# Whole 128x128 float32 products for the last two batches' linear attention, in front of two feed-forward layers

## Chip, cores and metric

The kernel runs on one core of a Trainium2 chip. The metric is the device time of one execution in microseconds, as the median of several runs. Engines are named as in the profile: PE is TensorE's products and PEld its weight loads, DVE is VectorE, ACT is ScalarE, POOL is GpSimd, SP is the engine that issues most DMAs.

## What is computed

Random-feature attention for 4 batches, 8 heads, 576 positions and a head size of 64 with 128 features, then two feed-forward layers over all 2304 tokens (512 to 2048 to 512), everything in float32:

```python
def phi(x):
    proj = np.einsum('bhsd,md->bhsm', x, omega)
    h = proj - np.sum(x * x, axis=-1, keepdims=True) / 2.0
    h = h - np.max(h, axis=-1, keepdims=True)
    return np.exp(h) / np.sqrt(m)
kv = np.einsum('bhsm,bhsd->bhmd', k_p, v)
z = np.sum(k_p, axis=2)
num = np.einsum('bhsm,bhmd->bhsd', q_p, kv)
den = np.einsum('bhsm,bhm->bhs', q_p, z)[..., None] + 1e-06
attn = num / den
# then x @ w_in, h * clip(h + 3, 0, 6) / 6, @ w_out
# then x @ w_in, h * sigmoid(1.702 h), @ w_out
```

## The kernel before

**Tiles.** The 576 positions of a head are four blocks of 128 (R = 4) and 64 leftover positions (SL). Values carry a 65th column of ones (D + 1 = 65), so that the product of key features and values gives `kv` and `z` together, and the product of query features with that gives numerator and denominator together. Leftover positions of the two heads of a pair share one tile: the first head's keys (and values, in `lv`) on rows 0 to 63, the second's on rows 64 to 127.

**Stages.** The first batch's attention runs alone at the start. From then on the attention of batch n + 1 is cut into steps (`att_steps`), and the steps are put between the products of the first feed-forward layer for batch n: `side()`, called in the middle and at the end of every chunk of `emit_h` and `emit_o`, takes steps from the list `todo` at an even pace. So the third batch's attention lies within the layer's work on the second batch (about 193 to 295 us), the fourth's within that on the third (about 307 to 417 us). The first layer's products with w_in are L459, those with w_out L510, both 128x128 weights against 512 columns in reduced float32 split into high and low parts. The second layer (L811, L828, L942) starts near 558 us. A scheduler that simulates the engines sets the order of the instructions on each engine from the order in which the kernel gives them, and each engine then runs in that order.

**Steps of one batch's attention.** For h from 0 to 9, in this order: `PJ(h)` projects keys and queries of head h (L259, two row halves side by side) and takes maxima and exponentials; after it, for h = 0, `PL` does so for the leftovers and, for h = 2, `QTL` transposes the leftover queries of all heads (L293); `NU(h - 2)` makes numerators and denominators (L354) and, for odd heads, those of the pair's leftovers (L363), then normalises (`norm`: L376, L380, L381 on DVE); `QT(h - 1)` transposes query features (L337) and `KV(h - 1)` makes the key-value sum (four blocks at L315, leftovers at L323, copied by ACT at L331); for odd h from 3 on, `XT` transposes the finished pair (L392) and splits it for the feed-forward layer (L247, L248); at the end `XTL` transposes the leftovers (L399).

**What the change touches.** Key-value sums and numerators are done in column halves: `KV` loads weight columns 0 to 63 and 64 to 127 of the features as two products that write PSUM rows 0 to 63 and 64 to 127, and `NU` does the same with the query features. The leftover product of `KV` takes 64 rows and 64 columns at a time. The accumulators come from a ring of four PSUM banks (`bank`, pool `psp`) that `emit_h` and the attention share. `load_left` issues the leftover loads on SP (`lqk`, and `lv` at L119); `kv` tiles come from a ring of four.

Of the kernel before, what the change touches and what calls it, by code (L numbers as in the profile page):

```python
# [8 lines left out]
F32 = mybir.dt.float32  # L9
# [13 lines left out]
def performer_moe_kernel(  # L23
# [13 lines left out]
    nc = tc.nc  # L37
# [4 lines left out]
    B, NPAIR, P = qk.shape[:3]  # L42
    H = 2 * NPAIR
    R = v.shape[4]
    D = omega.shape[0] // 2
    M = omega.shape[1]
    SM = R * P
    SL = lv.shape[1] // 2
# [6 lines left out]
    TAIL = 12  # L55
    WARM = 8
    FIRST = 4
    HELD = 8
    LOOK = 5
    PREP = 9  # L60
# [23 lines left out]
    def bank(shape, name):  # L84
        n_ps[0] += 1
        if banks[0] == "acc" or banks[0] == "both" and n_ps[0] % 2:
            return acc.tile(shape, F32, tag="acc", name="acc")
        return psp.tile(shape, F32, tag="ps", name="ps")
# [6 lines left out]
        return stack  # L95


    qkv = {}
    lqkv = {}
    last_load = [None]  # L100
# [13 lines left out]

    def load_left(b):
        a = at.tile([P, NPAIR, P], F32, tag="lqk", bufs=1, name="lqk")
        vl = at.tile([P, NPAIR, D + 1], F32, tag="lv", bufs=2, name="lv")
        nc.sync.dma_start(out=a, in_=lqk[b])
        nc.sync.dma_start(out=vl, in_=lv[b])  # L119
        lqkv[b] = (a, vl)  # L120

    w_dram = ((w1_in, w1_out), (w2_in, w2_out))
# [124 lines left out]
        nc.scalar.copy(hi, ps)  # L247
        nc.vector.tensor_tensor(out=lo, in0=ps, in1=hi.bitcast(F32), op=ALU.subtract)  # L248

    HALVES = (slice(0, D), slice(D, 2 * D))  # L250

    def project(a, ps):

        last = None
# [17 lines left out]
    class Att:  # L272


        def __init__(self, b, x, xl):
            self.b, self.x, self.xl = b, x, xl
            self.e, self.kv, self.xt, self.feat, self.qt = {}, {}, {}, {}, {}

        def leftover(self, i, j):
# [27 lines left out]
            return self.e[h][:, r % 2, 2 * j + r // 2]  # L307

        def KV(self, h):
            i, p0 = h // 2, 64 * (h % 2)  # L310
            vv = qkv[self.b, i][1]
            ps = bank([P, D + 1], "ps")
            for r in range(R):
                for m0 in (0, 64):
                    nc.tensor.matmul(  # L315
                        out=ps[m0:m0 + 64, :],
                        lhsT=self.feature(h, 0, r)[:, m0:m0 + 64],
                        rhs=vv[:, h % 2, r, :],
                        start=(r == 0),
                        stop=False,  # L320
                    )
            for m0 in (0, 64):
                nc.tensor.matmul(  # L323
                    out=ps[m0:m0 + 64, :],
                    lhsT=self.leftover(i, 1)[p0:p0 + SL, m0:m0 + 64],
                    rhs=self.vl[p0:p0 + SL, i, :],
                    start=False,
                    stop=True,
                )
            kv = at.tile([P, D + 1], F32, tag="kv", bufs=4, name="kv")  # L330
            nc.scalar.copy(kv, ps)  # L331
            self.kv[h] = kv

# [11 lines left out]
        def NU(self, h):  # L345
            i = h // 2
            t = self.qt.pop(h)
            kv = self.kv[h]
            if h % 2 == 0:
                self.xt[i] = at.tile([P, R, 2, D], F32, tag="xt", bufs=1, name="xt")  # L350
            ps = bank([P, 6, D + 1], "ps")
            for r in range(R):
                for s0 in (0, 64):
                    nc.tensor.matmul(  # L354
                        out=ps[s0:s0 + 64, r, :],
                        lhsT=t[:, r, s0:s0 + 64],
                        rhs=kv,
                        start=True,
                        stop=True,
                    )  # L360
            if h % 2:
                for e in range(2):
                    nc.tensor.matmul(  # L363
                        out=ps[0:SL, R + e, :],
                        lhsT=self.qtl[:, i, 64 * e:64 * e + SL],
                        rhs=self.kv.pop(2 * i + e),
                        start=True,
                        stop=True,
                    )
            self.norm(ps[:, 0:R, :], self.xt[i][:, :, h % 2, :], P, R)  # L370
            if h % 2:
                self.norm(ps[0:SL, R:R + 2, :], self.xln[:, i], SL, 2)

        def norm(self, ps, dst, np_, n):
            d = at.tile([P, R, 1], F32, tag="den", bufs=3, name="den")
# [29 lines left out]
    def att_steps(a):  # L405
        b = a.b
        st = []
        for h in range(H + 2):
            if h < H:
                st.append(lambda h=h: a.PJ(h))  # L410
            if h == 0:
                st += [lambda: None] * 2 + [lambda: a.PL()]
            if h == 2:
                st.append(lambda: a.QTL())
            if 2 <= h:
                st.append(lambda h=h: a.NU(h - 2))
            if 1 <= h <= H:
                st.append(lambda h=h: a.QT(h - 1))
                st.append(lambda h=h: a.KV(h - 1))
                if h % 2 == 0:  # L420
                    st.append(("load", (h - 1) // 2))
            if 2 <= h and h % 2:
                st.append(lambda h=h: a.XT((h - 2) // 2))
        st.append(lambda: a.XTL())
        fin = []
        for s in st:
            if isinstance(s, tuple):
                i = s[1] + 2
                bb, i = b + i // NPAIR, i % NPAIR
                if bb < B:  # L430
                    prev = fin.pop()

                    def f(prev=prev, bb=bb, i=i):
                        prev()
                        load_pair(bb, i)
                        if i == 0:
                            load_left(bb)
                    fin.append(f)
            else:
                fin.append(s)  # L440
        return fin
# [8 lines left out]
    def emit_h(n, c, side):  # L450
        w = ws[0, "i", c].rearrange("p s (k f) -> p s k f", k=NK)
        for i, N in SEGS[n]:
            pool = lp if i == B else gp
            x = xblk[i]
            ps = psp.tile([P, N], F32, tag="ps", name="ps")
            m = 0
            for kk in range(NK):
                for wi, xi in ((0, 0), (0, 1), (1, 0)):
                    nc.tensor.matmul(  # L459
                        out=ps,  # L460
                        lhsT=w[:, wi, kk, :],
                        rhs=x[:, xi, kk, :],
                        start=(m == 0),
                        stop=(m == 3 * NK - 1),
                    )
# [13 lines left out]
            if i == n:  # L479
                late_at("next")  # L480
                late_at("gate")
            hgt[i, c] = s
            side()
# [155 lines left out]
    for n in range(WARM):  # L639
        nc.tensor.matmul(  # L640
            out=ps.rearrange("p a m -> p (a m)"),
            lhsT=zero_r,
# [119 lines left out]
    for u in range(len(units) + LAG):  # L762
        while fetches and fetches[0][0] <= u + AHEAD:
            fetch_w(0, *fetches.pop(0)[1:])
        if u < len(units):
            n, c = units[u]
            if c == 0 and n + 1 < B:
                xblk[n + 1] = new_x(n + 1)
                steps = att_steps(Att(n + 1, xblk[n + 1], xl))
                todo = steps[::-1]  # L770
                pace[:] = len(todo), 0, 8 * (n > 0)
            if (n, c) == (B - 2, NC - 1):
                while todo:
                    todo.pop()()
                actx.close()
                lp = ctx.enter_context(
                    tc.tile_pool(name="lp", bufs=1, side="right", reuse_waits="tile")
                )
                xblk[B] = new_x(B)
                for kk in range(NK):  # L780
                    split_x(xl, xblk[B], kk)
            if n > 0:
                before_chunk(n, c)
            emit_h(n, c, side)
            if n == 0:
                convert_next(2, min(c + 2, NC), *(att.feat[H - 1] if c == 0 else ()))
            if (n, c) == (B - 1, PREP):
                assert n_late[0] == len(late)
                prep, _ = x_ops(0, wp, "w")
            if c == NC - 1:  # L790
                while todo:
                    todo.pop()()
        if u >= LAG:
            emit_o(*units[u - LAG], side)
# [343 lines left out]
```

## Time and profile before

| | us |
|---|---|
| median of 3 runs | 927.65 (926.71 to 927.83) |
| the profiled execution | 928.67 |
| its span, first to last instruction | 926.9 |
| TensorE products busy | 909.7 |
| TensorE weight loads busy | 772.0 |
| VectorE / ScalarE / GpSimd busy | 553.1 / 477.8 / 320.9 |

Times in rows count from the start of the span. A group of rows gives engine, line, operation, out<-in by the kernel's names, weight rows*columns, shapes, and how many. Products are pipelined: one record is longer than the step from its start to the next one's start, so steps are read from starts, or from a group's length less its last record.

### The profile page before, as it was taken

The numbers are of one execution on the slowest core, as the hardware profiler recorded it, in microseconds if no ns is written. First come the engines' busy times: TensorE is split into PE (matmuls) and PEld (weight loads), VectorE is DVE, ScalarE is ACT, GpSimd is POOL, SyncE is SP. The second block draws the span as 40 slices with busy tenths as digits, with TensorE's granted clock in tenths as the row PEclk, the third lists the DMA queues.
The fourth block names the chain that finished last, engine by engine and source line by source line (L and its number), as shares of the span: only waits on it lengthen the run. The fifth ranks groups of instructions, "written<-read, shape, count | busy, mean of one in ns | idle before, by whom it ended". The sixth has DMA issues, their size and how long they took to land.

```text
span 926.9 us, 16527 instructions
## 1 busy us (share of the span) xinstructions
PE 909.7 (98%) x6346; PEld 772.0 (83%) x6346; DVE 553.1 (60%) x944; ACT 477.8 (52%) x969; POOL 320.9 (35%) x251
## 2 busy tenths in 40 slices
PE   8899999999999999999999999999999999999997
PEld 6677777787777787778888888778999888899997
DVE  5877787463754836557563433776875443377653
ACT  6877676375664776646543333444544323244443
POOL 0122222054736557364772112884000244420000
PEclk9999999999999999999999999999999999999999
DMA  7677679687888998676866436999889544566572
GB/s 243 205 240 262 220 259 308 240 302 262 290 280 284 340 307 296 238 266 247 294 216 227 136 112 238 355 404 309 273 295 328 196 171 160 179 185 184 169 262 92
DMA packets 75167, 228.77 MB, mean 247 GB/s; under 512 B 7504, under 2 KB 13264, under 8 KB 75088
## 3 DMA queue, kind: packets, MB, share of 16 engines
q1 hardware_dynamic: 74928, 227.45, 71.5%
q8 instruction: 50, 0.82, 0.4%
q10 hardware_dynamic: 160, 0.26, 0.1%
q14 instruction: 29, 0.24, 0.1%
HBM read 164.77 MB, written 62.91 MB: 246 GB/s over the span
## 4 chain that ended last, share of the span: by engine, by line
PE 87%; DVE 5%; ACT 4%; DMA 2%; POOL 1%; issue 1%; DVEq 0%; SPq 0%; ACTq 0%
PE o L510 21%; PE ps L459 20%; PE o L942 20%; PE h L811 14%; PE ps L259 3%; PE hl L828 2%; ACT e L267 2%; PE ps L315 1%; PE ps L354 1%; PE ps L337 1%; DVE w L204 1%; DVE mx L265 1%; DMA fac<-xf 1%; DVE wtop L189 1%; PE ps L392 1%
## 5 line engine op out<-in xcount | busy, mean ns | idle before, releaser
L459 PE MATMUL ps<-x,wss 128*128 128x512 f32 x768 | 195.1, 399 | 0.9 <-ACT wss L207 0.6
L942 PE MATMUL o<-wss,gs 128*128 128x256 f32 x1536 | 185.2, 283 | 0.1
L942 PEld LDWEIGHTS o<-wss,gs 128*128 128x128 f32 x1536 | 184.5, 191 | 0.9 <-DVE gs L913 0.5
L459 PEld LDWEIGHTS ps<-x,wss 128*128 128x128 f32 x768 | 140.8, 189 | 33.4 <-ACT wss L207 2.0
L811 PE MATMUL h<-xo,wss 128*128 128x512 f32 x672 | 160.3, 394 | 1.0 <-DVE t L844 0.9
L811 PEld LDWEIGHTS h<-xo,wss 128*128 128x128 f32 x672 | 124.2, 188 | 28.9 <-DVE t L844 1.7
L196 POOL TENSOR_TENSOR w<-w,wpow 128x1024 f32<-128x1024 f32 x32 | 69.6, 2175 | 207.3 <-DVE wpow L193 166.4
L471 DVE SCALAR_TENSOR_TENSOR ga<-ga,ps 128x512 f32<-128x512 f32 (+1 forms) x80 | 49.7, 630 | 135.1 <-ACT ga L470 135.1
L852 POOL TENSOR_TENSOR g<-g,c 128x512 f32<-128x512 f32 x48 | 64.6, 1348 | 171.5 <-ACT g L851 171.3
L510 PE MATMUL o<-gs,wsh 128*128 128x512 f32 (+1 forms) x480 | 112.6, 377 | 0.8 <-ACT gs L475 0.8
L912 ACT CAST gs<-g 128x512 fp32r<-128x512 f32 x112 | 69.4, 621 | 85.1 <-PE o L942 79.3
L510 PE MATMUL o<-gs,wss 128*128 128x512 f32 (+1 forms) x480 | 110.4, 375 | 0.1
L221 POOL TENSOR_TENSOR wsn<-w,wsn 128x512 fp32r<-128x512 f32 x64 | 88.6, 1399 | 59.4 <-ACT wsn L220 58.4
L913 DVE TENSOR_TENSOR gs<-g,gs 128x512 fp32r<-128x512 f32 x112 | 79.7, 715 | 47.9 <-ACT gs L912 45.0
L470 ACT ACTIVATE ga<-ps,three 128x512 f32<-128x512 f32 (+1 forms) x80 | 51.2, 648 | 101.2 <-PE ps L459 100.8
L510 PEld LDWEIGHTS o<-gs,wsh 128*128 128x128 f32 x480 | 82.5, 188 | 18.0 <-ACT gs L475 1.1
L510 PEld LDWEIGHTS o<-gs,wss 128*128 128x128 f32 x480 | 82.2, 188 | 15.7 <-ACT gs L475 0.3
L476 DVE TENSOR_TENSOR gs<-ga,gs 128x512 fp32r<-128x512 f32 (+1 forms) x80 | 58.6, 742 | 18.4 <-ACT gs L475 17.0
L267 ACT ACTIVATE e<-ps,mx 128x128 f32<-128x128 f32 x220 | 61.4, 397 | 14.7 <-DVE mx L265 14.7
L851 ACT ACTIVATE g<-c 128x512 f32<-128x512 f32 x48 | 30.3, 632 | 62.7 <-DVE c L844 62.7
L475 ACT CAST gs<-ga 128x512 fp32r<-128x512 f32 (+1 forms) x80 | 46.0, 580 | 26.9 <-DVE ga L471 26.9
L204 DVE TENSOR_TENSOR w<-w,wtop 128x512 f32<-128x512 f32 x64 | 54.1, 890 | 7.4 <-POOL w L196 7.4
(127 smaller groups left out, 1084.1 us busy)
## 6 DMA issues: line engine op xcount, KB each, us to landing
wss<-left SPq DMA_DIRECT2D x64, 512.0 KB, 3.9
wss<-ws0i SPq DMA_DIRECT2D x48, 512.0 KB, 5.2
wraw<-in_w_in_dram SPq DMA_DIRECT2D x32, 512.0 KB, 5.6
wraw<-in_w_out_dram SPq DMA_DIRECT2D x32, 512.0 KB, 6.5
left<-wsn SPq DMA_DIRECT2D x32, 512.0 KB, 3.8
wss<-ws0o SPq DMA_DIRECT2D x24, 512.0 KB, 4.7
ws0i<-wss SPq DMA_DIRECT2D x16, 512.0 KB, 3.4
wss<-sumsa SPq DMA_DIRECT2D x16, 512.0 KB, 4.0
```

Of the source, the lines that this page charges most:

```text
L196: nc.gpsimd.tensor_tensor(out=w, in0=w, in1=q, op=ALU.mult)
L204: nc.vector.tensor_tensor(out=wj, in0=wj, in1=a[:, j * DM:(j + 1) * DM], op=ALU.add)
L221: nc.gpsimd.tensor_tensor(out=s[:, :, 1], in0=t, in1=s[:, :, 0].bitcast(F32), op=ALU.subtract)
L267: act = nc.scalar.activation(out=e[:, r, :], in_=ps[:, r, :], func=AF.Exp, bias=mx[:, r:r + 1])
L459: nc.tensor.matmul(out=ps, lhsT=w[:, wi, kk, :], rhs=x[:, xi, kk, :], start=(m == 0), stop=(m == 3 * NK - 1),)
L476: gate[1] = nc.vector.tensor_tensor(out=s[:, 1, :], in0=g, in1=s[:, 0, :].bitcast(F32), op=ALU.subtract)
L510: nc.tensor.matmul(out=ps[:, e, :], lhsT=w[:, wi, cols], rhs=s[:, gi, :], start=(c == 0 and m == 0 and per == 1), stop=(c == NC - 1 and m ...
L811: nc.tensor.matmul(out=ps, lhsT=s[:, wi, q, :], rhs=xop[q, op][:, xi], start=(first and m == 0), stop=(m == 5), skip_group_check=not first,)
L852: mul = eng.tensor_tensor(out=g, in0=g, in1=src, op=ALU.mult)
L912: split_ins[0] = nc.scalar.copy(s[:, 0], g)
L913: split_ins[1] = nc.vector.tensor_tensor(out=s[:, 1], in0=g, in1=s[:, 0].bitcast(F32), op=ALU.subtract)
L942: last_row[0] = nc.tensor.matmul(out=out, lhsT=s[:, gi, d * P:(d + 1) * P], rhs=w[:, wi, :], start=(start and m == 0), stop=(stop and m == 2),
```

## The change

For batches from `WHOLE` = 2 on (the third and the fourth), `KV` multiplies all 128 feature columns at once, and its leftover product takes all 128 rows: the other head's rows meet zeros in the values. For that the leftover values of a pair lie in two tiles `lvs`, one per parity of the batch, with a place for each head of a pair; both are zeroed once by GpSimd behind the fifth chunk of the first batch, and the values are loaded into them by two DMAs of 64 rows. `NU` multiplies 128 positions at once. The leftover numerators leave `NU` and become the step `NL`, four heads each, behind `NU(3)` and `NU(7)`, with one normalisation over four heads; the ring of `kv` grows from 4 to 10 for it. The first two batches keep their column halves.

```diff
+    WHOLE = 2
+    lvs = [at.tile([P, 2, NPAIR, D + 1], F32, name=f"lv{k}") for k in range(2)]
     def load_left(b):
...
+            vl = lvs[b % 2]
+            for e, rows in enumerate(HALVES):
+                nc.sync.dma_start(out=vl[rows, e], in_=lv[b, rows])
     def KV(self, h):
...
+            if self.whole:
+                cols, rows, vl = (slice(0, P),), slice(0, P), self.vl[:, h % 2, i, :]
+            else:
+                cols, rows = HALVES, HALVES[h % 2]
+                vl = self.vl[rows, i, :]
             for r in range(R):
-                for m0 in (0, 64):
+                for m in cols:
                     nc.tensor.matmul(
-                        out=ps[m0:m0 + 64, :],
-                        lhsT=self.feature(h, 0, r)[:, m0:m0 + 64],
+                        out=ps[m, :],
+                        lhsT=self.feature(h, 0, r)[:, m],
...
-            kv = at.tile([P, D + 1], F32, tag="kv", bufs=4, name="kv")
+            kv = at.tile([P, D + 1], F32, tag="kv", bufs=10, name="kv")
     def NU(self, h):
...
-                for s0 in (0, 64):
-                    nc.tensor.matmul(
-                        out=ps[s0:s0 + 64, r, :],
-                        lhsT=t[:, r, s0:s0 + 64],
+                for s in (slice(0, P),) if self.whole else HALVES:
+                    nc.tensor.matmul(out=ps[s, r, :], lhsT=t[:, r, s], rhs=kv, start=True, stop=True)
-            if h % 2:
+            if h % 2 and not self.whole:
...
+        def NL(self, q):
+            ps = bank([SL, 4, D + 1], "ps")
+            for n in range(4):
+                i, e = 2 * q + n // 2, n % 2
+                nc.tensor.matmul(
+                    out=ps[:, n, :],
+                    lhsT=self.qtl[:, i, 64 * e:64 * e + SL],
+                    rhs=self.kv.pop(4 * q + n),
+                    start=True,
+                    stop=True,
+                )
+            self.norm(ps, self.xln[:, 2 * q:2 * q + 2].rearrange("p i h d -> p (i h) d"), SL, 4)
     def att_steps(a):
...
+            if a.whole and h in (5, 9):
+                st.append(lambda h=h: a.NL((h - 5) // 4))
...
+            if (n, c) == (0, 4):
+                for vl in lvs:
+                    nc.gpsimd.memset(vl, 0.0)
```

## Rows read from the trace of the kernel before

**Rows 1.** The page's head: busy us, share of the span, records of each engine.

```profile
PE 909.7 (98%) x6346; PEld 772.0 (83%) x6346; DVE 553.1 (60%) x944; ACT 477.8 (52%) x969; POOL 320.9 (35%) x251
```

**Rows 2.** Stretches: length, busy us by engine, granted clock, DMA share, GB/s.

```profile
190.00:243.00 53.00, 53.00 (x420) 42.38 (x422) 30.36 (x52) 33.04 (x83) 24.43 (x21) 1.00 0.82 285
...
365.00:417.00 52.00, 50.98 (x400) 39.99 (x399) 27.25 (x54) 27.45 (x61) 29.40 (x26) 1.00 0.74 261
417.00:557.00 140.00, 140.00 (x793) 121.94 (x793) 71.71 (x105) 63.12 (x116) 61.28 (x50) 1.00 0.59 206
```

**Rows 3.** Waits of TensorE from 190 to 425 us: total, times, longest.

```profile
PE ps L337 <- DVE ga L471: 1.1, 1, 1.1
PE ps L392 <- DVE den L376: 1.0, 1, 1.0
```

**Rows 4.** TensorE's groups by line and shape, 190 to 425 us: busy, mean ns | idle.

```profile
L354 PE MATMUL ps<-kv,qpt 128*64 128x65 f32 x256 | 11.0, 228 | 0.0
L315 PE MATMUL ps<-v,e 128*64 128x65 f32 x256 | 11.0, 227 | 0.0
```

**Rows 5.** Single lines, 190 to 425 us: ns min/median/max, first to last start.

```profile
L315 PEld LDWEIGHTS ps<-v,e x256: 132/138/139, 204.2 to 409.8; 128*64 128x64 f32 x128
L315 PE MATMUL ps<-v,e x256: 218/222/272, 204.2 to 409.9; 128*64 128x65 f32 x128
...
L259 PEld LDWEIGHTS ps<-omt,qk x240: 182/188/189, 195.8 to 395.0; 64*128 64x128 f32 x120
L259 PE MATMUL ps<-omt,qk x240: 271/272/374, 195.9 to 395.1; 64*128 64x128 f32 x120
...
L337 PEld LDWEIGHTS ps<-ident,e x64: 138/140/143, 200.7 to 407.5; 128*128 128x128 f32 x64
...
L459 PEld LDWEIGHTS ps<-x,wss x324: 186/188/192, 201.2 to 406.8; 128*128 128x128 f32 x162
```

**Rows 6.** Timeline of TensorE around one key-value group, narrow windows: start, length.

```profile
262.81 0.39 PE L510 MATMUL o<-gs,wsh 128*128 128x512 f32 x1
...
263.13 0.69 PE L315 MATMUL ps<-v,e 128*64 128x65 f32 x16
...
263.75 0.33 PE L323 MATMUL ps<-lv,el 64*64 64x65 f32 x4
264.01 0.96 PE L459 MATMUL ps<-x,wss 128*128 128x512 f32 x3
...
264.35 0.86 PE L459 MATMUL ps<-x,wss 128*128 128x512 f32 x3
```

**Rows 7.** Timeline of TensorE: an odd head's numerators, behind a projection.

```profile
268.73 1.16 PE L259 MATMUL ps<-omt,qk 64*128 64x128 f32 x14
269.82 0.69 PE L354 MATMUL ps<-kv,qpt 128*64 128x65 f32 x16
270.33 0.40 PE L363 MATMUL ps<-kv,qtl 128*64 128x65 f32 x4
270.66 0.55 PE L337 MATMUL ps<-ident,e 128*128 128x128 f32 x3
```

**Rows 8.** Timeline of TensorE: a key-value group with a projection behind it.

```profile
205.08 1.16 PE L259 MATMUL ps<-omt,qk 64*128 64x128 f32 x16
```

**Rows 9.** The second layer's output products, 643 to 700 us, as rows 5.

```profile
L942 PE MATMUL o<-wss,gs x477: 278/283/288, 642.8 to 699.9; 128*128 128x256 f32 x159
```

**Rows 10.** Timeline of TensorE at the end of the fourth batch's attention.

```profile
414.89 0.40 PE L363 MATMUL ps<-kv,qtl 128*64 128x65 f32 x4
416.30 0.63 PE L392 MATMUL ps<-ident,xt 128*128 128x128 f32 x4 [1.02 <-DVE den L376]
```

**Rows 11.** GpSimd's groups by line and shape, whole span, as rows 4.

```profile
masks.py:197 POOL MEMSET ident<- 128x128 f32 x1 | 0.2, 204 | 0.3 <-POOLq L1125 0.3
```

**Rows 12.** Timeline of GpSimd in the first batch's chunks.

```profile
92.03 2.14 POOL L196 TENSOR_TENSOR w<-w,wpow 128x1024 f32<-128x1024 f32 x1 [6.02 <-DVE wpow L193]
```

**Rows 13.** DMA issues: queue, count, KB each, median us to landing.

```profile
lv<-in_lv_dram SPq DMA_DIRECT2D x4, 130.0 KB, 5.2
```

More of the change, by code (lines that the diff above doesn't have):

```diff
@@ L95, in behind @@
         return stack
+    HALVES = (slice(0, D), slice(D, 2 * D))
+    lvs = [at.tile([P, 2, NPAIR, D + 1], F32, name=f"lv{k}") for k in range(2)]
     qkv = {}
@@ L116, in load_left @@
         a = at.tile([P, NPAIR, P], F32, tag="lqk", bufs=1, name="lqk")
-        vl = at.tile([P, NPAIR, D + 1], F32, tag="lv", bufs=2, name="lv")
         nc.sync.dma_start(out=a, in_=lqk[b])
-        nc.sync.dma_start(out=vl, in_=lv[b])
+        if b < WHOLE:
+            vl = at.tile([P, NPAIR, D + 1], F32, tag="lv", bufs=2, name="lv")
+            nc.sync.dma_start(out=vl, in_=lv[b])
+        else:
+            vl = lvs[b % 2]
+            for e, rows in enumerate(HALVES):
+                nc.sync.dma_start(out=vl[rows, e], in_=lv[b, rows])
         lqkv[b] = (a, vl)
@@ L248, in split @@
         nc.vector.tensor_tensor(out=lo, in0=ps, in1=hi.bitcast(F32), op=ALU.subtract)
-    HALVES = (slice(0, D), slice(D, 2 * D))
     def project(a, ps):
@@ L276, in __init__ @@
             self.b, self.x, self.xl = b, x, xl
+            self.whole = b >= WHOLE
             self.e, self.kv, self.xt, self.feat, self.qt = {}, {}, {}, {}, {}
@@ L309, in KV @@
         def KV(self, h):
-            i, p0 = h // 2, 64 * (h % 2)
+            i = h // 2
             vv = qkv[self.b, i][1]
             ps = bank([P, D + 1], "ps")
+            if self.whole:
+                cols, rows, vl = (slice(0, P),), slice(0, P), self.vl[:, h % 2, i, :]
+            else:
+                cols, rows = HALVES, HALVES[h % 2]
+                vl = self.vl[rows, i, :]
             for r in range(R):
-                for m0 in (0, 64):
+                for m in cols:
                     nc.tensor.matmul(
-                        out=ps[m0:m0 + 64, :],
-                        lhsT=self.feature(h, 0, r)[:, m0:m0 + 64],
+                        out=ps[m, :],
+                        lhsT=self.feature(h, 0, r)[:, m],
                         rhs=vv[:, h % 2, r, :],
@@ L321, in KV @@
                     )
-            for m0 in (0, 64):
+            for m in cols:
                 nc.tensor.matmul(
[L324 to L328, printed above, removed]
+                    out=ps[m, :], lhsT=self.leftover(i, 1)[rows, m], rhs=vl, start=False, stop=True
                 )
-            kv = at.tile([P, D + 1], F32, tag="kv", bufs=4, name="kv")
+            kv = at.tile([P, D + 1], F32, tag="kv", bufs=10, name="kv")
             nc.scalar.copy(kv, ps)
@@ L352, in NU @@
             for r in range(R):
-                for s0 in (0, 64):
-                    nc.tensor.matmul(
-                        out=ps[s0:s0 + 64, r, :],
-                        lhsT=t[:, r, s0:s0 + 64],
[L357 to L360, printed above, removed]
-            if h % 2:
+                for s in (slice(0, P),) if self.whole else HALVES:
+                    nc.tensor.matmul(out=ps[s, r, :], lhsT=t[:, r, s], rhs=kv, start=True, stop=True)
+            if h % 2 and not self.whole:
                 for e in range(2):
@@ L370, in NU @@
             self.norm(ps[:, 0:R, :], self.xt[i][:, :, h % 2, :], P, R)
-            if h % 2:
+            if h % 2 and not self.whole:
                 self.norm(ps[0:SL, R:R + 2, :], self.xln[:, i], SL, 2)
+        def NL(self, q):
[10 more added lines that the diff above has]
+            self.norm(ps, self.xln[:, 2 * q:2 * q + 2].rearrange("p i h d -> p (i h) d"), SL, 4)
         def norm(self, ps, dst, np_, n):
```

## The prediction

> **What bounds the kernel now.** I read the head of the page first: TensorE is busy in 909.7 of 926.9 us [rows 1]. A busy TensorE may still be a slow one, so the next view is the table of stretches around the third and fourth batches' attention, which runs inside the first feed-forward layer of the second and third batches: about 193 to 295 us for the third, 307 to 417 us for the fourth. From 190 to 243 us TensorE has no idle time at all, from 365 to 417 us 50.98 of 52, at a granted clock of 1.00 (the 2.4 GHz level) [rows 2]. The waits of TensorE between 190 and 425 us are short: 1.1 us once before a query transpose, 1.0 us once at the end of the fourth batch [rows 3]. What the change adds to or takes from TensorE's stream there therefore moves the end one for one, except inside those two waits. From 417 to 557 us it is busy all of 140 us [rows 2], and over the span it misses only 17, so little behind swallows a delay. The case is a sum over TensorE's own steps.
>
> **Prices of a step, from single insertions.** The two batches have 256 records each of key-value products and of numerators [rows 4]: 2 batches x 8 heads x 4 blocks x 2 halves are 128 products, so a float32 product is two passes, each with its own weight load. Four prices follow.
> - A pass of a column half. One key-value group has 16 records in 0.69 us [rows 6]. Less the last one's 0.22 us and the first load's 0.05, seven steps of a pair remain, of 0.058 us each. The two halves run side by side: L363, which has one half alone, also needs 0.058 a pass (270.33 to 270.66 for four, less the turn of 0.09 [rows 7]).
> - The turn into another tile shape. The last L510 product starts at 262.81 and holds the array for the 0.23 us that is the step of its kind (three records from 264.35 in 0.86 us, the last of them 0.39 long); the half-column group starts at 263.13 [rows 6]. 0.09 us go by with nothing streaming. Then the first load lies open: the first record is longer than the median, 272 against 222 ns for 64 columns (0.05) and 374 against 272 for 128 columns (0.10) [rows 5]; 0.11 for the wide product that follows (264.01 to 264.35 against 0.23) [rows 6]. A turn thus costs 0.148 into a half-column group or a transpose and 0.200 into a product with 128 weight columns.
> - The group's inside. A key-value group has 8 pairs, a turn to the 64x64 leftover and 2 more pairs: 0.464 + 0.148 + 0.116 = 0.728. With the turns in and out 1.076. Check: from 262.81 to 264.35 are 1.54 us, less two L-512 steps of 0.23 leaves 1.08 [rows 6].
> - A pass of 128x128 with 65 columns: no such float32 product is in the trace, and it decides the case. It streams no longer than a half (0.058), but loads 128 columns. Load time goes by columns here: the load record lasts 138 ns for 64 columns and 188 for 128, whether the tile has 64 or 128 rows [rows 5], and the open first load is 0.05 against 0.10. In the projection (128 weight columns, two row halves side by side) a pair takes (1.16 - 0.27 - 0.10) / 7 = 0.112 us [rows 8]. I take 0.112, the nearest row. Its floor from the rows is the open load, 0.10 to 0.105; its upper end is the 0.120 of L942, (699.9 - 642.8) / 476, the shortest step of a full 128x128 product [rows 9]. A transpose's load lasts only 140 ns for 128 columns [rows 5], the one row that speaks for a fast load, but it is another operation; 0.058 is kept as a rival.
>
> The Trainium skill has a rule against this change: "TensorE: Matmul & The Clock Gate", Part 3 (Packing small matmuls), says that a weight load overlaps products in flight only where the row group differs; two 128x128 products share theirs, so load and stream would add. L942's 0.120 with a 188 ns load record under each product is too short for that, so the trace disagrees.
>
> **The change part by part** (third and fourth batch together).
> - Key-value sums, 16 groups. Fourteen stand between full-shape work. Before 1.076; after, 4 blocks and one leftover product over all 128 rows, 10 passes x 0.112 = 1.120, no turn: +0.044 each, +0.60 with those that end in a transpose (the exit saved is 0.05 smaller, but so is the last pass). Two are followed by a projection [rows 8], where the turn out stays: 9 x 0.112 + 0.058 + 0.200 = 1.266, +0.19 each, +0.38. Sum **+0.98**.
> - Numerators of even heads, 8 groups. Before 0.148 + 0.464 + 0.200 = 0.812; after 8 x 0.112 = 0.896. **+0.67**.
> - Numerators of odd heads, 8 groups. Before, with two leftover products on one column half at 0.058 a pass (four records): 0.148 + 0.464 + 0.236 + 0.200 = 1.048. Six stand right behind a projection [rows 7]; they keep a turn in, now with the longer load: 0.200 + 0.896 = 1.096, +0.29 in all. The two of head 7 come from wide products: 0.896, -0.15 each. In the fourth batch that one only ends a little earlier in front of a wait (below) and counts nothing. Sum **+0.14**.
> - Leftover numerators as steps of their own, 4 groups of four heads. They stay in one column half, without a partner, and now have both turns to themselves: 0.148 + 8 x 0.058 + 0.200 = 0.812. Two stand right behind a numerator group, whose last pass is then 0.058 and not 0.112. The last one, at the end of the fourth batch, falls into the wait of 1.02 us between L363 and the transposes L392, which wait for VectorE's normalisation [rows 10], and is free; if that cover went, it would cost its 0.81. Sum 3 x 0.81 - 0.11 = **+2.33**.
> - Beside the path: VectorE has two normalisations of 64x4 in place of four of 64x2 per batch, and it is busy only 60% of the span [rows 1]. The two POOL memsets (520 elements a row each) fall behind the fifth chunk of the first batch; one of 128 elements took 204 ns [rows 11], four times that is 0.8, and POOL idles about 6 us before each of its multiplications there [rows 12]; later in the queue stand those multiplications, which have the slack. SP issues one more load of leftover values for each of the two batches; the load is issued whole heads ahead and its landing took 5.2 us at the median [rows 13], the tiles are free, so nothing queued behind it on SP waits. The deeper ring of sums only frees. All at nothing; uncovered they would be worth the 0.8 us twice, and they can't gain.
>
> Sum: 0.98 + 0.67 + 0.14 + 2.33 = **+4.1 us**. 276 passes carry the open price: at 0.105 the sum is +2.2, at 0.120 +6.3. The profiled execution took 928.67 us, 926.9 of it span, and stands 1.02 above the median of the runs. 928.67 + 4.1 = 932.8 for it, and 927.65 + 4.1 = **931.7** for the median.
>
> **The rivals.**
> - The full load is quick enough to hide under the stream: a pass of 0.058. For it: the transpose's 140 ns load [rows 5]; against it: every plain product's 188. The sum falls by 276 x 0.054 = 14.9 to -10.8, about **917**. The mechanism decides from the point where a pass is below 0.097 us (4.1 / 276 = 0.015 less than 0.112); below that the kernel is faster than before. The skill's page of the same title, section "Back-to-back issue gap", gives a formula by moving columns alone, which would put a pass here at 0.057, and a sustained 81 ns for 128 columns, which would put the sum at -4.4 (an estimate from that page); both belong to this rival.
> - Load and stream in series, 0.112 + 0.058 = 0.170 a pass: +16.0 more, about **948**. Against it speaks L942 [rows 9].
> - The added time is absorbed: the instruction order is made anew, the leftover step takes the next accumulator bank of the ring in front of the query transpose that waited 1.1 us [rows 3], and the drains land where TensorE waited. At most those 2.1 us [rows 3], half of which I have already counted, and the low pass price of 0.105: +0 to +1.5, about **928.5**. That also covers a change that does less than it says.
> - The same ring makes a new wait: the leftover step holds a bank through VectorE's normalisation, and transposes or projections behind it stall as the one at 245 us did, 1.1 us each, in two places: +2.2, about **934**, inside the range.
>
> **How the numbers follow.** Forecast (with the new waits) 0.72, absorbed 0.13, fast load 0.12, series 0.03. The range takes the forecast's ends (0.105 to 0.120 a pass: 929.8 to 934.0, and up to 2 us of reordered waits on top) and the absorbed case below: 927.0 to 936.0, which leaves out the two extremes and some of the forecast's tail. What a measurement of this kernel can tell from no change is about 0.2%, 1.9 us: faster is below 925.8, slower above 929.5. Faster: the fast load, 0.12, and 0.01 of the absorbed. Same: most of the absorbed, 0.11, and 0.05 of the forecast. Slower: the rest, 0.71.
>
> **What the profile after would show.** If right: the key-value and numerator products of those batches read 128*128, 10 and 8 records to a group, in steps near 0.112 us, with load records near 188 ns; no gap of 0.09 us before or after them between wide products; four leftover groups 128*64 of 8 records, each with a turn on both sides; TensorE still without idle time from 190 to 417 us, and that stretch some 4 us longer. Steps near 0.06 would refute the load price, steps near 0.17 the overlap. If the steps are 0.112 and the time is still the same or lower, the order of the work or the waits have moved, and the sum misses that. It would also be wrong if the gap of a turn does not vanish between float32 and reduced float32 products of the same shape; transposes next to wide products show none today.

## The result and the profile after

The changed kernel takes 933.67 us (933.31 to 934.43, four runs) against 927.35 for the kernel before: a ratio of 1.0068, 95% interval 1.0052 to 1.0084, so 4.8 to 7.8 us slower. The forecast was 931.7, slower. The profiled execution took 933.89 us, its span 932.1, against 926.9.

The page's head and, of the waits of TensorE from 190 to 430 us, all there are (compare [rows 1, 3]); the last line is the third wait of the kernel before, beside the two of [rows 3]:

```profile
PE 916.4 (98%) x6058; PEld 784.8 (84%) x6058; DVE 549.2 (59%) x932; ACT 477.8 (51%) x969; POOL 320.0 (34%) x253
...
PE ps L408 <- DVE xt L397: 0.6, 1, 0.6
...
PE ps L259 <- DVE ga L471: 0.2, 1, 0.2
```

TensorE has 288 records fewer and 6.7 us more to do; its waits in the stretch have shrunk from 2.3 us to 0.6. The work itself has grown. Where, TensorE's groups by line and shape from 190 to 430 us show (busy, mean ns | idle), and below them weight loads of the same stretch (answers to [rows 4, 5]). L327 and L335 are now the key-value sums, L362 the numerators, L381 the leftover numerators, L265 the projection, L345 and L408 transposes, L477 and L528 the feed-forward products:

```profile
L362 PE MATMUL ps<-kv,qpt 128*128 128x65 f32 x128 | 16.6, 273 | 0.0
L327 PE MATMUL ps<-v,e 128*128 128x65 f32 x128 | 16.2, 270 | 0.0
...
L327 PEld LDWEIGHTS ps<-v,e 128*128 128x128 f32 x128 | 16.3, 191 | 1.0
L362 PEld LDWEIGHTS ps<-kv,qpt 128*128 128x128 f32 x128 | 16.2, 191 | 1.3
```

Half as many records, and 16.6 and 16.2 us busy where 11.0 were [rows 4]: a record of a whole product costs three times what one of a half did. Its weight load lasts 191 ns, as every plain 128-column load, not 138.

One key-value group between feed-forward products, from the timeline of TensorE in narrow windows (start, length; the answer to [rows 6]):

```profile
222.92 0.39 PE L528 MATMUL o<-gs,wss 128*128 128x512 f32 x1
...
223.16 1.00 PE L327 MATMUL ps<-v,e 128*128 128x65 f32 x8
223.99 0.39 PE L335 MATMUL ps<-lv,el 128*128 128x65 f32 x2
...
224.50 0.63 PE L477 MATMUL ps<-x,wss 128*128 128x512 f32 x2
```

L528 streams until 222.92 + 0.23 = 223.15 and the group starts at 223.16: no drain. From 222.92 to the second L477 behind the group, at 224.50, are 1.58 us; less two steps of 0.23 leaves 1.12, ten passes of 0.112. The same measure was 1.08 in halves.

### The profile page after: what moved, and what is told of

It is laid out like the page before. It is cut to its first block, busy times and chain, and to the rows that moved or that the text cites. A ratio compares the mean times of both kernels' runs of the same rounds, so it can differ in the third digit from the quotient of the medians.

```text
span 932.1 us, 15944 instructions
## 1 busy us (share of the span) xinstructions
PE 916.4 (98%) x6058; PEld 784.8 (84%) x6058; DVE 549.2 (59%) x932; ACT 477.8 (51%) x969; POOL 320.0 (34%) x253
## 4 chain that ended last, share of the span: by engine, by line
PE 89%; ACT 4%; DVE 4%; DMA 1%; POOL 1%; issue 1%; DVEq 0%; ACTq 0%
PE o L528 21%; PE ps L477 21%; PE o L963 19%; PE h L832 14%; PE ps L265 3%; PE hl L849 2%; PE ps L362 2%; PE ps L327 2%; ACT e L273 2%; PE ps L345 1%; DMA wss<-sumsa 1%; DVE mx L271 1%; DMA wss<-sumsd 1%; DVE w L212 1%; PE ps L408 1%
## 5 line engine op out<-in xcount | busy, mean ns | idle before, releaser
L477 PE MATMUL ps<-x,wss 128*128 128x512 f32 x768 | 195.1, 399 | 0.9 <-ACT wss L215 0.4
L477 PEld LDWEIGHTS ps<-x,wss 128*128 128x128 f32 x768 | 140.6, 189 | 33.2 <-ACT wss L215 2.0
L528 PE MATMUL o<-gs,wsh 128*128 128x512 f32 (+1 forms) x480 | 112.9, 378 | 0.8 <-ACT gs L493 0.8
L528 PE MATMUL o<-gs,wss 128*128 128x512 f32 (+1 forms) x480 | 110.5, 375 | 0.1
L528 PEld LDWEIGHTS o<-gs,wsh 128*128 128x128 f32 x480 | 82.3, 188 | 17.4 <-ACT gs L493 1.1
L528 PEld LDWEIGHTS o<-gs,wss 128*128 128x128 f32 x480 | 81.9, 188 | 15.4 <-ACT gs L493 0.3
L212 DVE TENSOR_TENSOR w<-w,wtop 128x512 f32<-128x512 f32 x64 | 51.6, 851 | 7.5 <-POOL w L204 7.4
```

Of the source, the lines that this page charges most:

```text
L212: nc.vector.tensor_tensor(out=wj, in0=wj, in1=a[:, j * DM:(j + 1) * DM], op=ALU.add)
L477: nc.tensor.matmul(out=ps, lhsT=w[:, wi, kk, :], rhs=x[:, xi, kk, :], start=(m == 0), stop=(m == 3 * NK - 1),)
L528: nc.tensor.matmul(out=ps[:, e, :], lhsT=w[:, wi, cols], rhs=s[:, gi, :], start=(c == 0 and m == 0 and per == 1), stop=(c == NC - 1 and m ...
```

## The experiments

Twelve kernels ran, each timed beside the kernel before on the same chip (medians of before: 928.26 for the first four, 927.90 for the next, 927.53 for the last). To set traces side by side I use one stretch throughout: from the 217th to the 577th record of the first layer's w_in product, 180.3 to 420.3 us in the kernel before, which holds all the work of the two batches. "Turns" counts where two neighbouring records of TensorE differ in tile shape, "projections" the separate groups of L259, both counted over the timeline of that stretch of the one profiled execution. A change of time in microseconds, where one is given with an interval, is the ratio applied to the median of the kernel before.

| kernel | stretch us | turns | projections | timed, ratio to before (95%) |
|---|---|---|---|---|
| before | 240.08 | 124 | 23 | 1 |
| the change | 245.71 | 68 | 26 | 1.0068 (1.0052 to 1.0084) |
| kv_whole | 241.10 | 78 | 23 | 1.0002 (0.9993 to 1.0011) |
| nu_whole | 243.76 | 110 | 25 | 1.0031 (1.0020 to 1.0042) |
| nl_alone | 241.89 | 137 | 25 | 1.0011 (1.0002 to 1.0020) |
| nu_left_inside | 243.47 | 112 | 22 | 1.0036 (1.0024 to 1.0049) |
| kv_130 | 246.28 | 66 | 25 | 1.0058 (1.0045 to 1.0072) |
| empty_steps | 243.94 | 125 | 23 | 1.0013 (1.0004 to 1.0022) |
| ring_step | 245.38 | 129 | 25 | 1.0048 (1.0034 to 1.0062) |
| halves_rows | 238.30 | 108 | 23 | 0.9973 (0.9961 to 0.9984) |
| rows_from1 | 237.84 | 108 | 23 | 0.9969 (0.9958 to 0.9981) |
| rows_all | 238.95 | 108 | 23 | 0.9968 (0.9957 to 0.9978) |
| rows_joined | 240.91 | 90 | 24 | 1.0022 (1.0013 to 1.0031) |
| rows_joined_pj | 244.09 | 79 | 23 | 1.0008 (0.9999 to 1.0017) |

The stretch is one execution of each kernel and the ratio several. The profiled executions of empty_steps and rows_all took 2.1 and 2.4 us more than the medians of theirs, and the stretch of rows_joined_pj holds eight w_out products (1.8 us) more than the others. Where the two columns differ, the ratio decides on the time; the stretch serves to say where it went.

**kv_whole: the key-value sums alone.** Out of the change, `NU` goes back to halves and `NL` goes:

```diff
-                for s in (slice(0, P),) if self.whole else HALVES:
+                for s in HALVES:
...
-            if a.whole and h in (5, 9):
-                st.append(lambda h=h: a.NL((h - 5) // 4))
```

> Only the key-value sums of the third and fourth batch are whole; numerators keep their column halves and their leftovers. Theory (a whole pass costs its load, 0.112 us, and a group loses its two turns): 16 groups at +0.02 to +0.19 each, +1.0 us over the kernel before, about 928.4; counting the turns in the new instruction order gives +1.0 as well. Rival (the added time of the full change comes from the leftover step and its waits, whole passes are cheap at 0.058): -7.7 us, about 919.6.

Measured: +0.2 us (-0.6 to +1.0); in the stretch +1.02, with the same waits as before. The stretch gives the forecast's +0.98 almost to the digit; in the timed runs it lies at the upper edge of the interval and is not shown apart from no change. The rival's -7.7 is out.

**nu_whole: the numerators and their leftover steps alone.** Out of the change, `KV` and the loads of `lv` go back:

```diff
-            if self.whole:
-                cols, rows, vl = (slice(0, P),), slice(0, P), self.vl[:, h % 2, i, :]
-            else:
-                cols, rows = HALVES, HALVES[h % 2]
-                vl = self.vl[rows, i, :]
+            cols, rows = HALVES, HALVES[h % 2]
+            vl = self.vl[rows, i, :]
```

> Only the numerators are whole, with the leftover numerators in two steps of four heads; key-value sums as before. Theory: +0.8 for numerators and +2.3 for the leftover steps, +3.1 us by groups; the new order separates the numerators from the projections and splits projections more often, by its count of turns +4.8, about 932.2. Rival (key-value sums carry the added time): under +1.5.

Measured: +2.9 us (1.9 to 3.9), in the stretch +3.7. The groups' sum gave +3.1, the count of turns +4.8; the wait of 1.1 us in front of a query transpose [rows 3] is not in this trace, which is about the way from +4.8 to +3.7.

**nl_alone: only the leftover steps**, every product in halves (`KV` and the loads go back as in nu_whole):

```diff
-                for s in (slice(0, P),) if self.whole else HALVES:
+                for s in HALVES:
                     nc.tensor.matmul(out=ps[s, r, :], lhsT=t[:, r, s], rhs=kv, start=True, stop=True)
```

> Every product stays in column halves; only the leftover numerators are taken out of the numerator groups into two steps of four heads. Theory: 4 new groups with two turns each, 4 x 0.81, against 16 x 0.118 inside the old groups: +1.4 us, +0.6 if the last is hidden in the wait at the end of the fourth batch; with the turns counted in its order +2.6, less 0.8 hidden, +1.8. Rival (the step itself is free, its bank makes waits): the waits of TensorE grow by as much as the time.

Measured: +1.0 us (0.2 to 1.9), in the stretch +1.8. TensorE's waits between 190 and 425 us fell from 2.3 to 1.1, so the rival is wrong: the steps cost by their turns (137 against 124), and the waits do not grow with them (one new one, of 0.5 us, is among the 1.1). This kernel also has 25 projections where 23 were, although nothing about a projection was touched.

**nu_left_inside: whole numerators, leftovers inside the odd heads' groups**, no steps of their own (`KV` as in nu_whole):

```diff
-            if a.whole and h in (5, 9):
-                st.append(lambda h=h: a.NL((h - 5) // 4))
...
-            if h % 2 and not self.whole:
+            if h % 2:
```

> Only the numerators are whole, and the leftover numerators stay in column halves inside the odd heads' groups, without steps of their own. Theory: even heads +0.7; an odd head's group gets a turn into the column halves for its two leftovers (0.148 + 0.236 + 0.200 beside the whole passes), +0.58 each behind a projection and +0.38 for head 7, +4.2; together +4.9 us, +4.6 by the turns in its order, no more projections split than before. Rival (the steps of their own are what makes the change slow): less than nu_whole, under +2.9.

Measured: +3.3 us (2.2 to 4.5), in the stretch +3.4: a miss by 1.3 to 1.6. Here, too, the 1.1 us wait is gone; of the waits of [rows 3] only the one at the end is left. Against nu_whole the difference is not clear: taking the leftovers out of the groups neither saved nor cost a measurable amount by itself.

**kv_130: twice the columns in each whole key-value pass.** The products of the change run against both heads' values; half of the sums goes unused:

```diff
-                        rhs=vv[:, h % 2, r, :],
+                        rhs=vv[:, :, r, :] if wide else vv[:, h % 2, r, :],
...
-            nc.scalar.copy(kv, ps)
+            nc.scalar.copy(kv, ps[:, h % 2] if wide else ps)
```

> The full change, but the whole key-value products of the third and fourth batch run against the values of both heads of the pair: 130 columns where 65 did; half of the sums goes unused. Theory (a whole pass lasts as long as its 128-column load, 0.112 us, and 130 columns swept in about 0.108 fit under it): steps stay at 0.112 to 0.116 and the time stays that of the change, +5.9 us over the kernel before by the turns of its order. Rival (load and stream add up in a whole pass, or the pass goes by its columns): 160 passes x 0.054 = +8.6 more, +14.5.

Measured: +5.4 us (4.2 to 6.7). The timeline of TensorE around one group:

```profile
222.51 1.05 PE L328 MATMUL ps<-v,e 128*128 128x130 f32 x8
223.40 0.39 PE L336 MATMUL ps<-lv,el 128*128 128x130 f32 x2
...
223.85 0.63 PE L478 MATMUL ps<-x,wss 128*128 128x512 f32 x2
```

From 222.51 to the second L478, at 223.85, less the 0.23 of the first are 1.11 us, ten passes of 0.11 again. Doubling the columns costs nothing, so a pass of 65 columns is set by its load, and load and stream do overlap. The Trainium skill's page "TensorE: Matmul & The Clock Gate", Part 3 (Packing small matmuls), under which loads of the same row group wait for the products in flight, does not hold here: by it, 130 columns would have come on top. Its section "LDWEIGHTS (loading the stationary operand)", which sets a load by its columns alone (by its formula, an estimate, 0.107 us for 128), agrees with the 0.112.

**empty_steps: the list's length.** The kernel before, with two steps that do nothing at the places of `NL`:

```diff
                 st.append(lambda h=h: a.NU(h - 2))
+            if b >= 2 and h in (5, 9):
+                st.append(lambda: None)
```

> The kernel before with two empty steps in the third and fourth batch's list, where the change has its leftover steps: only the places of the other steps move. Theory (the part of the change's +6.3 us beyond the forecast's +4.1 is eight more turns around projections, and comes of the work that is moved, not of the list's length): the count of turns in its order gives +0.3 us, between -0.5 and +0.8. Rival (two more steps in the list are enough to split projections): +1.5 us or more.

Measured: +1.2 us (0.4 to 2.0), in the stretch +3.9. Neither theory had this. The number of projections stays at 23, so the list's length does not split them; but at the start of the fourth batch's attention there are two new waits. The timeline of TensorE there (in brackets the idle time before and what ended it), and the table of stretches (length, busy us and records of TensorE, its loads, VectorE, ScalarE and GpSimd, granted clock, DMA share, GB/s):

```profile
320.25 1.16 PE L259 MATMUL ps<-omt,qk 64*128 64x128 f32 x14 [1.17 <-ACT el L267]
321.33 0.66 PE L337 MATMUL ps<-ident,e 128*128 128x128 f32 x4
322.58 1.13 PE L315 MATMUL ps<-v,e 128*64 128x65 f32 x16 [0.59 <-DVE ga L473]
323.64 0.48 PE L323 MATMUL ps<-lv,el 64*64 64x65 f32 x4
324.05 5.38 PE L512 MATMUL o<-gs,wss 128*128 128x512 f32 x12
...
318.00:322.00 4.00, 2.82 (x23) 1.94 (x21) 1.78 (x4) 2.75 (x9) 3.73 (x4) 1.00 0.92 302
322.00:326.00 4.00, 3.42 (x25) 2.81 (x26) 2.41 (x4) 3.44 (x11) 2.96 (x3) 0.54 0.72 279
326.00:330.00 4.00, 4.00 (x13) 3.16 (x12) 0.00 (x0) 0.88 (x4) 3.20 (x5) 0.60 0.71 263
```

Twelve L512 products take 5.38 us, 0.43 apiece and not 0.23. Over the 8 us from 322 to 330 the granted clock was 0.54 and 0.60 on average, so mostly the lower of its two levels (1.2 GHz). Those products cost some 2.3 us more by it, the key-value group in front of them 0.6 (1.47 us from its start to theirs, where 0.88 [rows 6]). The stretch's +3.9 less these 2.9 is +1.0, close to the timed +1.2, so the median does not need the low clock of the profiled execution. That execution took 930.88 us, the longest of eleven, at a mean granted clock of 0.993 over the span, as in one other (930.88 too); in five of the eleven (927.87 to 929.72 us) the mean was 0.999, which has no room for such a stretch. What the +1.2 is made of there, no trace shows.

**ring_step: the accumulator bank.** Two added steps which take a bank from the ring and hardly do anything else:

```diff
+        def TAKE(self):
+            ps = bank([P, P], "ps")
+            nc.tensor.transpose(ps, ident, ident)
+            t = at.tile([P, P], F32, tag="take", bufs=1, name="take")
+            nc.vector.tensor_copy(t, ps)
...
+            if b >= 2 and h in (5, 9):
+                st.append(lambda: a.TAKE())
```

> The kernel before with two added steps in the third and fourth batch at the places of the leftover steps; each only takes an accumulator bank from the ring, transposes the identity into it (0.11 us on TensorE) and lets VectorE copy it out. Theory (taking a bank from the ring ahead of a projection, which needs two at once, splits projections, and each split costs a turn in and out, 0.4 us): 46 projection groups in its order where the kernels before and with empty steps have 44, +1.5 us by the turns and the four transposes, and in the trace two or three more turns into 64*128 than in empty_steps. Rival (the list's length alone does it): as empty_steps, +1.2, with no more turns into 64*128 than the kernel before.

Measured: +4.5 us (3.2 to 5.7), far more than +1.5. The trace has the same waits as empty_steps at the same place, and a low clock behind them, for a shorter time:

```profile
322.60 1.16 PE L259 MATMUL ps<-omt,qk 64*128 64x128 f32 x14 [1.29 <-ACT el L267]
323.68 0.66 PE L337 MATMUL ps<-ident,e 128*128 128x128 f32 x4
324.93 1.02 PE L315 MATMUL ps<-v,e 128*64 128x65 f32 x16 [0.59 <-DVE ga L479]
...
326.30 4.04 PE L518 MATMUL o<-gs,wss 128*128 128x512 f32 x12
...
324.00:328.00 4.00, 3.40 (x28) 2.64 (x26) 2.58 (x4) 3.25 (x10) 2.91 (x4) 0.64 0.82 297
```

So empty_steps, not the kernel before, is its measure. Against it the stretch is 1.44 us longer, but the low clock cost less here: the twelve products took 4.04 us and not 5.38, so that without the low clock it is some 2.9 us; by the ratios it is 3.3. In it are two projections more (25), four turns more and four transposes (4 x 0.11 = 0.44). The splits (0.6 us each, below) and the transposes make 1.6 of it; the rest is not placed. The rival (length alone) is wrong about the splits; the theory missed the waits.

**halves_rows: only the zero-padded leftovers.** All products stay in halves; the leftover product of the key-value sum keeps the tile shape of its group. Of the change's `KV`, with `NU` in halves and no `NL`:

```diff
             if self.whole:
-                cols, rows, vl = (slice(0, P),), slice(0, P), self.vl[:, h % 2, i, :]
+                cols, rows, vl = HALVES, slice(0, P), self.vl[:, h % 2, i, :]
```

> Column halves everywhere, as before; in the third and fourth batch only the leftover product of the key-value sum takes all 128 rows against zero-padded values, so that the group has no turn from 128*64 to 64*64 inside. Theory (a turn costs 0.09 of drain and 0.055 of open load): 16 x 0.148 = -2.4 us, about 925.0, with the instruction order unchanged. Rival (the turn inside a group is covered by the loads or the queue, or the longer contraction costs as much): 0.0.

Measured: -2.5 us (-1.5 to -3.6), faster than the kernel before; medians 926.05 against 928.26. One group of its timeline:

```profile
262.25 0.69 PE L327 MATMUL ps<-v,e 128*64 128x65 f32 x16
262.77 0.29 PE L335 MATMUL ps<-lv,el 128*64 128x65 f32 x4
262.98 2.34 PE L475 MATMUL ps<-x,wss 128*128 128x512 f32 x9
```

From the group's start to the next product's are 0.73 us where 0.88 were [rows 6]: the 0.15 of one turn, 16 times. (The stretch is shorter by only 1.8 us, because the waits in it came to 0.5 us more.) Here the Trainium skill's page "TensorEngine Tiling (Array Packing)", Key Properties, agrees: a change of tiling mode drains TensorE, a change of tile within a mode does not.

**rows_from1 and rows_all: the same in three and in four batches.** `WHOLE` is 1 and 0, and the two tiles are zeroed at the start:

```diff
-    WHOLE = 2
+    WHOLE = 1
...
+    for vl in lvs:
+        nc.gpsimd.memset(vl, 0.0)
```

> As halves_rows (column halves, the key-value leftovers over 128 rows against zero-padded values), from the second batch on, with both value tiles zeroed at the start. Theory: 24 x 0.148 = -3.6 us, the instruction order unchanged, about 924. Rival (in the second batch's stretch TensorE waits for converted weights, so a saved turn only lengthens a wait): -2.5, as halves_rows.

Measured: -2.9 us (-1.8 to -3.9), medians 924.86 against 927.53.

> As rows_from1, in all four batches. Theory: the first batch's attention runs alone and its key-value sum lies on the chain to the numerators, so that eight more turns go: up to -1.2 beyond rows_from1, -4.7 us, about 923. Rival (at the start the zeroing and two loads in place of one lie ahead of the first inputs, and other engines set the pace there): no better than rows_from1, or up to 1 us worse.

Measured: -3.0 us (-2.0 to -4.0), medians 924.25 against 927.53. Both are faster than the kernel before and the change. That the second batch adds something to halves_rows, and the first to rows_from1, lies within the intervals: neither is shown.

**rows_joined and rows_joined_pj: fewer turns by order.** On top of rows_from1, from the second batch on, numerators of one head and key-value sum of the next become one step (the edit below), then also the projection behind them:

```diff
+                    def both(h=h):
+                        if 2 <= h:
+                            a.NU(h - 2)
+                        a.KV(h - 1)
+                    st.append(both)
+                    st.append(lambda h=h: a.QT(h - 1))
```

> Column halves everywhere. From the second batch on the key-value leftovers take 128 rows against zero-padded values, as in halves_rows, and the numerators of head h - 2 and the key-value sum of head h - 1 are one step, with the query transposes behind it, so that two half-column groups share their turns. Theory (time goes with the turns): 24 x 0.148 = -3.6 us for the leftovers and -2.8 for 22 turns less in its order, -6.4 us, about 922. Rival (the joined step makes the sums or the transposes wait): no better than halves_rows, -2.5.

Measured: +2.0 us (1.2 to 2.9).

> As rows_joined, with the next head's projection in the same step behind the two half-column groups, so that they leave into the projection. Theory: 49 turns less than halves_rows in its order, -9 us beyond the -3.6 of the leftovers if nothing waits, -12 us; the waits for free accumulators grow, since five banks are asked for at once, so -6 to -12 us. Rival (the waits take it all): -2.5 or worse.

Measured: +0.7 us (-0.1 to +1.6). They miss the theory by 8.4 us and by 6.7 or more; both rivals, that waits would take it, were right. The turns did go, to 90 and 79, and waits took their place. Those of rows_joined from 190 to 425 us, and behind the longest of them the timeline of TensorE and the stretches, columns as above:

```profile
PE ps L486 <- issue: 2.0, 1, 2.0
PE ps L486 <- ACT e L276: 1.2, 1, 1.2
PE ps L330 <- ACT e L276: 1.1, 1, 1.1
PE ps L411 <- DVE den L395: 0.9, 1, 0.9
PE ps L365 <- ACT qpt L353: 0.6, 2, 0.3
...
279.19 4.38 PE L486 MATMUL ps<-x,wss 128*128 128x512 f32 x12 [1.96 <-issue]
...
278.00:282.00 4.00, 2.81 (x9) 2.34 (x10) 1.43 (x3) 1.05 (x5) 2.48 (x2) 0.81 1.02 402
282.00:286.00 4.00, 3.71 (x48) 2.99 (x46) 1.27 (x2) 2.28 (x4) 0.00 (x0) 0.77 0.65 248
```

Key-value sums (L330) now wait for the exponentials and numerators (L365) for the copied transposes, which steps of other work used to cover. What the wait of 2.0 us stands for, which the profile cannot name, stays open. Behind it the granted clock fell here as well, to 0.81 and 0.77 over two stretches, and twelve products took 4.38 us where 3.0 is usual; rows_joined_pj has two such places (0.57 from 248 to 252 us and from 292 to 296). So a part of what its stretch shows is clock, in that one execution.

## Why the prediction was right, and where it was short

- **What bounds** the stretch: right. In the stretch, every kernel whose products grew was slower, and the three that only lost turns were faster; timed, the same holds but for kv_whole, whose +1.0 is within the noise.
- **The price of a whole pass**, the number on which the case hung: 0.112 forecast, 0.112 measured, with loads of 191 ns. kv_130 shows why: the load sets it. The rivals of 0.058 (917 us) and of load and stream in series (948 us) are both out. The 0.057 that the prediction works out from the Trainium skill's formula is what that formula gives for 130 columns, a pass that sweeps its 65 twice; for 65 it would be 0.030, an estimate from that page, and further off.
- **The turns**: the gap around whole groups vanished, and between float32 and reduced float32 of the same shape there is none; halves_rows gives the price of one turn, 0.15, by itself.
- **Key-value sums**: +0.98 forecast, +1.02 in the stretch of kv_whole.
- **Numerators and leftover steps**: 0.81 + 2.33 = +3.1 forecast, +3.7 in the stretch of nu_whole, +2.9 timed.
- **The sum**: +4.1 forecast, +5.6 in the stretch and +6.3 (4.8 to 7.8) timed. The term that was mis-sized is the order of the work, which the sum took as unchanged. With it, the change would have 60 turns in the stretch; it has 68. Three more projections are split in two, and one more transpose of leftovers, each with a turn in and out. The timeline of TensorE in the change shows an undivided projection of sixteen records, then such a split, two records of a projection, a row of feed-forward products, the other fourteen:

```profile
309.07 1.16 PE L265 MATMUL ps<-omt,qk 64*128 64x128 f32 x16
310.17 3.06 PE L528 MATMUL o<-gs,wsh 128*128 128x512 f32 x12
313.16 0.49 PE L265 MATMUL ps<-omt,lqk 64*128 64x128 f32 x2
313.57 3.02 PE L528 MATMUL o<-gs,wss 128*128 128x512 f32 x12
316.52 1.16 PE L265 MATMUL ps<-omt,lqk 64*128 64x128 f32 x14
317.61 3.02 PE L477 MATMUL ps<-x,wss 128*128 128x512 f32 x12
```

  A split costs more than its two turns of 0.2. From a part's start to the next product are 0.41 us for two records and 1.09 for fourteen, together 0.40 more than the 1.10 of sixteen; with the 0.09 of drain before the added part and the 0.11 of open load behind it, 0.6 us. The part of two records is one product, whose two passes have no partner in the other row half beside them: 0.10 of open load, twice 0.11 and 0.09 of drain are its 0.41. Three splits are 1.8 us, the split transpose 0.3: 2.1 us in all.

  The splits come with a step that takes a bank of the ring for a product and a copy: 25 or 26 projections in each of the five kernels that have such a step (the change, kv_130, nu_whole, nl_alone, ring_step), 22 or 23 in the kernel before and the six others that keep the order of steps, empty_steps among them. That it is the bank, and not the product or the copy, is argued and not shown: a projection needs two banks at once, and with one taken its first product would go ahead alone.
- **The wait of 1.1 us** before a query transpose [rows 3] disappeared, -1.1; the forecast had it only as a rival's gain. 4.1 + 2.1 - 1.1 is 5.1, and 0.1 more comes of leftover steps that no longer stand right behind numerators. About 0.4 of the stretch's 5.6 us I cannot place.
- **The range** held the time partly by luck. Its room above the sum was meant for a dearer pass (0.120) and for 2 us of reordered waits; the pass was not dearer and the waits fell from 2.3 to 0.6 us. Split projections, which the prediction does not price, filled that room. The rival of a new wait behind the ring (934) has nearly the measured number and the wrong mechanism.
- **The cover at the end of the fourth batch** held. The timeline of TensorE there (answer to [rows 10]), and below it the numerators at that place in the kernel before:

```profile
419.01 1.00 PE L362 MATMUL ps<-kv,qpt 128*128 128x65 f32 x8
419.94 0.68 PE L381 MATMUL ps<-kv,qtl 128*64 128x65 f32 x8
421.20 0.66 PE L408 MATMUL ps<-ident,xt 128*128 128x128 f32 x4 [0.58 <-DVE xt L397]
...
414.37 0.69 PE L354 MATMUL ps<-kv,qpt 128*64 128x65 f32 x16
```

  From the numerators' start to the transposes are 2.19 us; before, they were 1.93, from 414.37 to 416.30 [rows 10]. The leftover step's 0.8 us cost 0.26, which the 0.2 of the third wait that went makes up for.
- **"Absorbed" and the list's place in time**: the prediction's rivals priced a new order at up to 2.1 us less, by waits that go, or 2.2 more, by waits that come. The wait that the first of them named did go, and the time rose all the same. empty_steps shows that the place of the steps alone is worth +1.2 us; the change itself has neither its waits nor its low clock at that place (its clock is 1.00 throughout the stretch). So that cost is not seen in the change, though it could have been.
- **Zeroing, the extra loads, the smaller normalisations**: at nothing. halves_rows, which has the same zeroing and the same loads, came out at -2.5 us where its turns alone give -2.4. No run takes the normalisations by themselves.

## What to carry to other kernels

Price a small product by the larger of its stream and its weight load: with 65 columns two side-by-side column halves (0.058 us a pair of passes) cost half of one whole product (0.112 a pass), because their loads run side by side, too, and only the turns of the tile shape speak for the whole one. Take those turns away in another way: padding a small leftover with zeros so that it keeps its group's shape was worth 2.5 to 3 us here, while whole products lost more than the turns gave back. And in a kernel whose order comes from a scheduler, count turns and waits anew in the order that results: four steps that do no more than take a bank of the shared ring, transpose once into it and copy it out cost 4.5 us (ring_step), as much as the whole sum of the forecast; 1.2 of it came with empty steps at the same places.

## What was not expected of the hardware

- A pass of a whole float32 product takes 0.11 us with 65 and with 130 columns alike (kv_130).
- A split projection costs 0.6 us and not the 0.4 of its two turns: the product that goes ahead alone takes its two passes of 0.11 us without a partner in the other row half (the change).
- Right behind two waits of 1.2 to 1.3 and of 0.6 us, with a projection and a query transpose of TensorE between them, the granted clock was 0.54 (empty_steps) and 0.64 (ring_step) over 4 us, and behind one wait of 2.0 us 0.81 and 0.77 (rows_joined); the wait of 1.1 us at 244 us in the kernel before left it at 1.00. The products there took 0.43 us in place of 0.23, which in empty_steps cost more (2.9 us, with the group in front) than the waits (1.8). It does not happen in every execution: five of the eleven of empty_steps have a mean granted clock of 0.999. What decides it stays open.
